# Attention and two feed-forward layers on one core: stores of parts one step later, behind the next step's loads

## The chip, the core and the metric

The kernel runs on one core of one Trainium2 chip. A core has five engines that run their own instruction streams in order and meet at semaphores: TensorE (PE in the rows; PEld is its weight load), VectorE (DVE), ScalarE (ACT), GpSimd (POOL) and SyncE (SP), which here issues every transfer between HBM and the core's memory. The metric is the device time of one execution in microseconds (us); lower is better.

## What is computed

Eight batches of eight heads of attention without a softmax over scores: q is softmaxed over its 64 features, k over its 576 positions, and the output is q (k^T v). The result, as 4608 tokens of 512 features, goes through two feed-forward layers of width 2048.

```python
def _attn_ref(q, k, v):                                   # (8, 8, 576, 64) each
    q_s = np.exp(q - np.max(q, axis=-1, keepdims=True))
    q_s = q_s / (np.sum(q_s, axis=-1, keepdims=True) + 1e-09)
    k_s = np.exp(k - np.max(k, axis=2, keepdims=True))
    k_s = k_s / (np.sum(k_s, axis=2, keepdims=True) + 1e-09)
    kv = np.einsum('bhsd,bhse->bhde', k_s, v)
    return np.einsum('bhsd,bhde->bhse', q_s, kv).astype(np.float32)

x = attn_out.transpose(0, 2, 1, 3).reshape(4608, 512)
h = x @ w_in;  x = (h - np.tanh(h)) @ w_out               # first layer
h = x @ w_in                                              # second layer, with a rational function
P = a[0] + a[1]*h + a[2]*h**2 + a[3]*h**3
Q = 1.0 + abs(b[0])*abs(h) + abs(b[1])*h**2
out = (P / (Q + 1e-6)) @ w_out
```

## The kernel before

Values are split in two parts, high and low, so that a product is three matmuls (high x high, high x low, low x high). The tokens are cut into nine blocks of 512 (NBLK), the layer's width into 16 slices of 128 (KF); a step is one slice of one block.

**The stages.** Up to some 140 us the attention of the first block is made. Then come the 144 steps of the first layer (loop over n in STEPS, j = block, f = slice). In a step TensorE makes the first product of slice f (`first_product`) and the second product of the slice two steps back (`second_product1`), and in between pieces of the next block's attention. From some 930 us on the second layer runs over an order that is written out by hand (ORDER), on units that are loaded back from HBM.

**A step's code** issues, in this order: `front(work[n])`, the parts of the next block's attention that are due in this step, loads, VectorE, ScalarE and GpSimd work; the first product; `turn(work[n])`, their TensorE work; the tanh (L936), the subtraction t (L939), its high part gh (L327) and low part gl (L331); what follows the TensorE work; and last, from step 17 on, one piece of each "errand" in the list `todo`. Each engine runs its instructions in that order.

**The attention pieces.** For each head pair p = 0 to 3 of the next block: `kv_max` and `kv_squares` make maxima of k and store them in HBM (kd, L532); `kv_fetch` loads them back, spread over the partitions, into the tile ke (L538); `kv_join` takes the maximum (mx<-ke, L544), `kv_sub` subtracts it from k into ke (L473), `kv_exp` takes the exponential (L483), and `kv_mm` multiplies with v (kvps, L490). For p = 1 the load is due in step 5, L544 and L473 in step 6, L483 and L490 in step 7; for p = 2 in steps 8, 9 and 10. The tile ke exists once. The parts of q go through HBM in the same way (qd, L622; ql, L629), and q's result is written to the four quarters of the tile xr in steps 5, 8, 11 and 14.

**The errands.** One (`errands`) brings the second layer's weights: a fetch into a staging tile raw (three of them; L118, L120), decoding on ScalarE and VectorE, splitting into high part e (three tiles) and low part m (four), and stores to HBM (L221, L225). The others are `x2_units`, one for each block that the first layer has done: step 1 copies the block's result from the accumulators to two staging tiles, and in steps 1 to 8 seven units of it are made in eight pieces. Each unit is split: a copy to a new high tile (ScalarE, L356), a subtraction in place (GpSimd, L357), and the stores of both parts (SyncE, L359), which are issued right there:

```python
hi = two(new_hi())                                        # one of the decoder's three e tiles
ACT.copy(out=hi.bitcast(F32R), in_=x)
POOL.tensor_tensor(out=x.bitcast(F32R), in0=x, in1=f32(hi), op=ALU.subtract)
for i, t in enumerate((hi, x)):
    SP.dma_start(out=two(x2d[j][:, 2 * UNITS.index(m) + i]), in_=f32(t))
```

SyncE issues in program order: a transfer whose data isn't ready holds all that stand behind it.

Of the kernel before, what the change touches and what calls it, by code (L numbers as in the profile page):

```python
# [8 lines left out]
F32 = mybir.dt.float32  # L9
F32R = mybir.dt.float32r  # L10
# [5 lines left out]
ALU = mybir.AluOpType  # L16
AX = mybir.AxisListType

P = 128
NB = 512  # L20
# [23 lines left out]
def attention_moe_moe2_kernel(ctx, tc, q, k, v, w1, w2, w3, w4, ca, cb, out):  # L44
# [21 lines left out]
    decp = tc.alloc_tile_pool(name="decp", bufs=2, side="right")  # L66
# [7 lines left out]
    PE, ACT, DVE, POOL, SP = nc.tensor, nc.scalar, nc.vector, nc.gpsimd, nc.sync  # L74

    def f32(ap):
        return ap.bitcast(F32)
# [111 lines left out]
    UNITS = (1, 5, 2, 6, 7, 4, 3)  # L189
    HALF = NB // 2  # L190

    def keep(key, n):
        parked[key] = dp.tile([P, n, NB], F32, tag=f"w{key}", name=f"w{key[0]}{key[1]}d")
        return parked[key]

    def errands():


        def raw():
            piece, t = staged.pop(0)  # L200
            return (t, *(dec_open(t) if wide else (None, t)))

        def whole(t, e, m):
            if wide:
                dec_join(e, m)
                return e, m
            e, m = (decp.tile([P, NB], x, tag=g, name=g, bufs=n) for x, g, n in ((U32, "e", 3), (U32, "m", 4)))
            POOL.tensor_copy(out=f32(m), in_=t)
            return e, m

        def high(e, m, n=NB):
            ACT.copy(out=e.bitcast(F32R)[:, 0:n], in_=f32(m)[:, 0:n])

        def low(e, m, n=NB):
            lo = m.bitcast(F32R)[:, 0:n]
            DVE.tensor_tensor(out=lo, in0=f32(m)[:, 0:n], in1=f32(e)[:, 0:n], op=ALU.subtract)

        def store(d, at, e, m, half):

            for i, x in enumerate((e, m)):  # L220
                SP.dma_start(out=d[:, UNITS.index(at), i * HALF:(i + 1) * HALF], in_=f32(x)[:, half * HALF:(half + 1) * HALF])  # L221

        def store_whole(d, e, m):
            for i, x in enumerate((e, m)):
                SP.dma_start(out=d[:, i], in_=f32(x))  # L225

        for f in range(0, KF, 2):
            d = keep(("a", f), len(UNITS))
            o = raw()
            fetch_w(1)  # L230
            yield
            e1, m1 = whole(*o)
            yield
            o = raw()
            high(e1, m1)
            fetch_w(1)
            yield
            e2, m2 = whole(*o)
            m4, m3 = (decp.tile([P, NB], U32, tag="m", name="m", bufs=4) for _ in range(2))
            x1, x2, x3, x4 = (f32(x) for x in (m1, m2, m3, m4))  # L240
            lo, hi = slice(0, HALF), slice(HALF, NB)
            POOL.tensor_tensor(out=x4[:, hi], in0=x1[:, lo], in1=x2[:, lo], op=ALU.subtract)
            POOL.tensor_tensor(out=x2[:, lo], in0=x2[:, lo], in1=x2[:, hi], op=ALU.add)
            POOL.tensor_tensor(out=x4[:, lo], in0=x2[:, lo], in1=x1[:, lo], op=ALU.subtract)
            POOL.tensor_tensor(out=x3[:, lo], in0=x1[:, hi], in1=x4[:, lo], op=ALU.subtract)
            yield
            high(e2, m2)
            low(e1, m1)
            store(d, 1, e1, m1, 0)
            store(d, 2, e1, m1, 1)  # L250
            yield
            low(e2, m2)
            store(d, 5, e2, m2, 0)
            store(d, 4, e2, m2, 1)
            e1 = decp.tile([P, NB], U32, tag="e", name="e", bufs=3)
            high(e1, m4)
            yield
            low(e1, m4)
            store(d, 6, e1, m4, 0)
            store(d, 7, e1, m4, 1)  # L260
            e2 = decp.tile([P, NB], U32, tag="e", name="e", bufs=3)
            high(e2, m3, HALF)
            yield
            low(e2, m3, HALF)
            store(d, 3, e2, m3, 0)
            for i in range(2):
                o = raw()
                yield
                e, m = whole(*o)
                fetch_w(1)  # L270
                yield
                high(e, m)
                yield
                low(e, m)
                store_whole(keep(("b", f + i), 2), e, m)

    todo = [errands()]

    def unpark(which, f):
# [26 lines left out]
    xr = xp.tile([P, KC, NB], F32, tag="xr", name="xr")  # L306
# [8 lines left out]
    def first_product(f):  # L315
        hps = ps_h.tile([P, NB], F32, tag="h", name="hps")
        for c in range(KC):
            wh, wl = wa(f, c)
            mm3(hps, wh, wl, xh[:, c, :], xl[:, c, :], c == 0, c == KC - 1)
        return hps  # L320
# [22 lines left out]
    def two(t):  # L343
        return t.rearrange("p (c x) -> p c x", c=2)

    def x2_units(j, k0, k1, ta, tb, new_hi):

        x11, x12, x21, x22 = k0[:, :, LO], k0[:, :, HI], k1[:, :, LO], k1[:, :, HI]
        ta, tb = two(ta), two(tb)

        def minus(o, a, b):
            POOL.tensor_tensor(out=o, in0=a, in1=b, op=ALU.subtract)

        def split(m, x):
            hi = two(new_hi())
            ACT.copy(out=hi.bitcast(F32R), in_=x)  # L356
            POOL.tensor_tensor(out=x.bitcast(F32R), in0=x, in1=f32(hi), op=ALU.subtract)  # L357
            for i, t in enumerate((hi, x)):
                SP.dma_start(out=two(x2d[j][:, 2 * UNITS.index(m) + i]), in_=f32(t))  # L359

        minus(ta, x12, x11)
        yield
        split(1, x11)
        minus(tb, x22, ta)
        yield
        split(5, ta)
        minus(x12, x22, x12)
        yield
        split(3, x22)
        yield  # L370
        split(7, x12)
        minus(ta, x21, tb)
        yield
        split(2, x21)
        yield
        split(6, tb)
        yield
        split(4, ta)

    identity = const.tile([P, P], F32, name="identity")  # L380
    coef = const.tile([P, 6], F32, name="coef")
# [278 lines left out]
    def front(todo):  # L660
        for fn, args in todo:
            if not isinstance(fn, tuple):
                fn(*args)
# [17 lines left out]
    for j in range(1, NBLK):  # L681
        for p in range(NPAIR):
            at = (j - 1) * KF + 3 * p
# [14 lines left out]
    with tc.manual_schedule():  # L698
# [56 lines left out]
        def second_product1(j, f, gh, gl):  # L755
            if f == 0:
                new_acc()
            wh, wl = wb(f)
            for m in range(4):
                c = slice(m * P, (m + 1) * P)  # L760
                mm3(acc[m], wh[:, c], wl[:, c], gh, gl, f == 0, f == KF - 1)

            def leave(acc=dict(acc)):
                halves = [xr[:, m:m + 2, :] for m in (0, 2)] if j == NBLK - 1 else [staging().rearrange("p (m t) -> p m t", m=2) for _ in range(2)]
                for m in range(4):
                    (DVE.tensor_copy if m % 2 else ACT.copy)(out=halves[m // 2][:, m % 2], in_=acc[m])
                if j < NBLK - 1:
                    todo.append(x2_units(
                        j, *halves, xr[:, 2, :], xr[:, 3, :],
                        lambda: decp.tile([P, NB], F32, tag="e", name="e", bufs=3),  # L770
                    ))

            return leave if f == KF - 1 else None

# [127 lines left out]
        for n in range(STEPS):  # L902
            j, f = n // KF, n % KF
            leave = None
            front(work[n])
            hps = first_product(f)
            if f == KF - 1 and j + 1 < NBLK:
                next_x()
# [3 lines left out]
            if n == last + 10:  # L912
                for errand in todo:
                    for _ in errand:
                        pass
                for pool in (att, bdp, decp, rawp):
                    pool.release()
                outp = ctx.enter_context(tc.tile_pool(name="outp", bufs=4, side="right"))
                rp = ctx.enter_context(tc.tile_pool(name="rp", bufs=2, side="right"))
                xup = ctx.enter_context(tc.tile_pool(name="xup", bufs=1, side="right"))  # L920
                units = [xup.tile([P, NB], F32R, tag=f"u{k}", name=f"u{k}") for k in range(12)]
                units += [w[:, c, :] for w in (xh, xl) for c in range(KC)]
                sums = xup.tile([P, NB], F32, tag="sums", name="sums")
                top = xup.tile([P, HALF], F32, tag="top", name="top")
                temp = xup.tile([P, NB], F32, tag="temp", name="temp")
                for u in range(6):
                    load_unit(0, u)
# [64 lines left out]
        for i in range(PAIRS + LAGS):  # L992
            for name, lag in ORDER:
                if 0 <= i - lag < PAIRS:
                    steps[name](i - lag)
                if i == 0 and name in ("P1", "P6"):
                    old()
            if i % 4 == 3:
                next(prep, None)

# [28 lines left out]
```

## Time and profile before

| | |
|---|---|
| median of 3 runs | 1704.54 us (1703.94 to 1705.71) |
| the profiled execution | 1705.21 us, its span 1703.4 us |
| busy, share of the span | TensorE 1644.1 us (97%), VectorE 1154.1 (68%), GpSimd 1035.3 (61%), ScalarE 1024.3 (60%) |
| TensorE busy, 0 to 140 us | 110.90 us |
| TensorE busy, 140 to 820 us | 660.90 us of 680 |
| TensorE busy, 820 to 920 us | 100.00 us of 100 |
| TensorE busy, 920 to 1703 us | 772.26 us of 783 |

The rows come from one profiled execution. A row of a view in order of time has a start (us from the span's start), a length, the engine and line, what is written and read, and in brackets how long the engine was idle before it and what ended that. "SPq" is an issue on SyncE's queue. Matmuls are pipelined and their ends are modelled.

### The profile page before, as it was taken

What the parts mean: (1) busy time and instruction counts of PE and PEld (TensorE: products, weight loads), DVE (VectorE), ACT (ScalarE), POOL (GpSimd) and SP (SyncE); (2) the same over time, 40 slices, a digit from 0 to 9 for tenths busy, and PEclk for the clock granted to TensorE, in tenths of its full rate; (3) what the DMA queues carried; (4) which work ended last, traced back from release to release, by engine and by line L of the source; (5) the groups of instructions that cost most, each with busy time, mean ns of one, the idle gap of its engine ahead of it and who ended that gap; (6) DMA issues with size and microseconds to landing.
All of it is one profiled execution on the core that took longest, in us unless ns stands there. A gap on an engine that the chain in (4) does not pass through costs nothing.

```text
span 1703.4 us, 25967 instructions
## 1 busy us (share of the span) xinstructions
PE 1644.1 (97%) x8776; PEld 1414.4 (83%) x8776; DVE 1154.1 (68%) x1948; ACT 1024.3 (60%) x1825; POOL 1035.3 (61%) x875
## 2 busy tenths in 40 slices
PE   5899999999999999999999999999999999999998
PEld 4677787888887788788888889998999999989996
DVE  7987566675756556654211778787878787878787
ACT  5675444544444444444332777777777777777775
POOL 4223626454553635446251888888888778878886
PEclk9999999999999999999999999999999999999999
DMA  8552654747375563735078676767675757676640
GB/s 221 169 169 87 191 161 150 203 125 218 117 198 148 153 200 121 204 93 167 13 237 300 251 268 221 271 213 271 211 272 198 260 198 260 200 258 204 218 153 26
DMA packets 246117, 323.69 MB, mean 190 GB/s; under 512 B 119008, under 2 KB 176352, under 8 KB 236768
## 3 DMA queue, kind: packets, MB, share of 16 engines
q1 hardware_dynamic: 245984, 322.03, 58.9%
q8 instruction: 69, 1.13, 0.3%
q14 instruction: 64, 0.52, 0.1%
HBM read 249.04 MB, written 72.93 MB: 189 GB/s over the span
## 4 chain that ended last, share of the span: by engine, by line
PE 75%; DVE 9%; DMA 5%; ACT 4%; issue 3%; POOL 2%; SPq 2%; ACTq 0%; POOLq 0%; DVEq 0%
PE acc L80 12%; PE acc L81 12%; PE acc L82 12%; PE z L826 12%; PE y L826 9%; PE hps L80 5%; PE hps L82 5%; PE hps L81 5%; DMA ke<-kd 2%; PE kvps L490 1%; DMA u<-x2d 1%; SPq L629 1%; DVE m L147 1%; DMA ql<-qd 1%; ACT m L133 1%
## 5 line engine op out<-in xcount | busy, mean ns | idle before, releaser
L331 POOL TENSOR_TENSOR gl<-t,gh 128x512 fp32r<-128x512 f32 x128 | 173.6, 1356 | 329.1 <-ACT gh L327 299.2
L327 ACT CAST gh<-t 128x512 fp32r<-128x512 f32 x128 | 79.9, 624 | 297.9 <-PE acc L82 122.0
L883 POOL TENSOR_TENSOR n<-n,r 128x512 f32<-128x512 f32 x144 | 186.7, 1296 | 97.2 <-ACT r L880 91.9
L883 POOL TENSOR_TENSOR n<-n,n 128x512 f32<-128x512 f32 x144 | 187.0, 1299 | 35.7 <-ACT n L867 35.7
L883 POOL TENSOR_TENSOR n<-n,h 128x512 f32<-128x512 f32 x144 | 187.6, 1303 | 9.7 <-DMA xh<-x2d 9.6
L939 DVE TENSOR_TENSOR t<-hps,t 128x512 f32<-128x512 f32 x128 | 87.5, 684 | 153.2 <-ACT t L936 152.7
L936 ACT ACTIVATE t<-hps 128x512 f32<-128x512 f32 x144 | 86.0, 597 | 95.7 <-PE hps L82 75.9
L837 ACT COPY sums<-z 128x256 f32<-128x256 f32 x144 | 53.9, 374 | 134.0 <-PE z L826 134.0
L863 ACT ACTIVATE n<-h,coef 128x512 f32<-128x512 f32 x144 | 116.9, 812 | 0.3 <-POOL n L883 0.3
L893 DVE CAST gh<-a 128x512 fp32r<-128x512 f32 x144 | 99.6, 692 | 16.8 <-PE acc L82 1.4
L896 DVE TENSOR_TENSOR gl<-a,gh 128x512 fp32r<-128x512 f32 x144 | 99.7, 692 | 15.2 <-DVE gh L893 0.5
L872 DVE SCALAR_TENSOR_TENSOR a<-h,absb,a 128x512 f32<-128x512 f32 x144 | 107.6, 747 | 3.0 <-ACT a L857 2.9
L889 DVE SCALAR_TENSOR_TENSOR a<-a,n 128x512 f32<-128x512 f32 x144 | 100.0, 695 | 14.0 <-POOL n L883 8.1
L857 ACT ACTIVATE a<-h,coef 128x512 f32<-128x512 f32 x144 | 100.7, 699 | 2.5 <-DVE gl L896 2.5
L886 DVE SCALAR_TENSOR_TENSOR a<-a,r 128x512 f32<-128x512 f32 x144 | 99.4, 690 | 0.8 <-ACT r L880 0.8
L875 ACT ACTIVATE r<-a,bias_q 128x512 f32<-128x512 f32 x144 | 97.3, 676 | 0.0
L880 ACT ACTIVATE r<-r 128x512 f32<-128x512 f32 x144 | 91.3, 634 | 4.6
L860 ACT ACTIVATE h<-h 128x512 f32<-128x512 f32 x144 | 89.4, 621 | 1.3 <-DMA xh<-x2d 0.8
L598 POOL TENSOR_TENSOR qe<-qe,qs 128x512 f32<-128x512 f32 x36 | 38.6, 1072 | 64.2 <-DVE qs L597 64.2
L490 PE MATMUL kvps<-vt,ke 128*128 128x130 f32 x320 | 49.1, 306 | 27.5 <-ACT ke L483 25.9
L490 PEld LDWEIGHTS kvps<-vt,ke 128*128 128x128 f32 x320 | 44.9, 212 | 35.2 <-ACT ke L483 31.7
L636 DVE TENSOR_TENSOR ql<-ql,qh 128x512 fp32r<-128x512 f32 x28 | 23.5, 841 | 74.2 <-ACT qh L635 74.2
(360 smaller groups left out, 5295.9 us busy)
## 6 DMA issues: line engine op xcount, KB each, us to landing
u<-x2d SPq DMA_DIRECT2D x78, 256.0 KB, 5.4
raw<-in_moe_w_in_dram SPq DMA_DIRECT2D x32, 512.0 KB, 4.4
raw<-in_moe_w_out_dram SPq DMA_DIRECT2D x32, 512.0 KB, 4.4
x2d<-e SPq DMA_DIRECT2D x56, 256.0 KB, 3.1
wa0h<-wa0d SPq DMA_DIRECT2D x9, 1024.0 KB, 5.1
wa1h<-wa2d SPq DMA_DIRECT2D x9, 1024.0 KB, 5.1
wa2h<-wa4d SPq DMA_DIRECT2D x9, 1024.0 KB, 5.2
wa3h<-wa6d SPq DMA_DIRECT2D x9, 1024.0 KB, 7.4
```

What stands on the lines that cost most here:

```text
L80: PE.matmul(o, lhi, rhi, start=start, stop=False)
L81: PE.matmul(o, lhi, rlo, start=False, stop=False)
L82: PE.matmul(o, llo, rhi, start=False, stop=stop)
L331: eng.tensor_tensor(out=gl, in0=g, in1=f32(gh), op=ALU.subtract)
L490: PE.matmul(ps[:, 0:2 * (D + 1)], e[:, g].rearrange("p h d -> p (h d)"), vs[:, :, g, :], start=g == 0, stop=g == G - 1,)
L826: PE.matmul(o, w, x[:, xc], start=m in (1, 5) and c == k == 0, stop=c == 1 and k == 2, skip_group_check=True,)
L857: ACT.activation(out=new(t, "a", ps_a), in_=t["h"], func=AF.Abs, scale=b0)
L863: ACT.activation(out=new(t, "n1"), in_=t["h"], func=AF.Identity, scale=a3, bias=a2)
L872: DVE.scalar_tensor_tensor(out=t["a"], in0=t["h2"], scalar=b1, in1=t["a"], op0=ALU.mult, op1=ALU.add)
L883: return lambda t: POOL.tensor_tensor(out=t[a], in0=t[a], in1=t[b], op=op)
L889: DVE.scalar_tensor_tensor(out=t["a"], in0=t["a"], scalar=2.0, in1=t["n0"], op0=ALU.subtract, op1=ALU.mult)
L896: DVE.tensor_tensor(out=t["g"][1], in0=t["a"], in1=f32(t["g"][0]), op=ALU.subtract)
```

## The change

The stores of the x2 units and of the second layer's weights are no longer issued where the parts are made. `send` puts them in a list, and `flush` issues that list: in each step right behind `front(work[n])`, that is behind the next step's attention loads; where all errands are finished (step `last + 10`), after each piece; and in the second layer's loop every fourth pair. The high parts of x2 no longer take the decoder's e tiles: of a block's seven, three go to quarters 0 and 1 of xr (`free`), and four to quarters of the two staging tiles whose units have been split before (x11, x22, x11 and x12).

```diff
+    late = []
+
+    def send(out, in_):
+        late.append(lambda: SP.dma_start(out=out, in_=in_))
+
+    def flush():
+        while late:
+            late.pop(0)()
...
             for i, x in enumerate((e, m)):
-                SP.dma_start(out=d[:, UNITS.index(at), i * HALF:(i + 1) * HALF], in_=f32(x)[:, half * HALF:(half + 1) * HALF])
+                send(d[:, UNITS.index(at), i * HALF:(i + 1) * HALF], f32(x)[:, half * HALF:(half + 1) * HALF])
...
             for i, x in enumerate((e, m)):
-                SP.dma_start(out=d[:, i], in_=f32(x))
+                send(d[:, i], f32(x))
...
-    def x2_units(j, k0, k1, ta, tb, new_hi):
+    def x2_units(j, k0, k1, ta, tb, free):
...
-        def split(m, x):
-            hi = two(new_hi())
+        def split(m, x, hi=None):
+            hi = two(free()) if hi is None else hi
             ACT.copy(out=hi.bitcast(F32R), in_=x)
-            POOL.tensor_tensor(out=x.bitcast(F32R), in0=x, in1=f32(hi), op=ALU.subtract)
+            POOL.tensor_tensor(out=x.bitcast(F32R), in0=x, in1=hi, op=ALU.subtract)
             for i, t in enumerate((hi, x)):
-                SP.dma_start(out=two(x2d[j][:, 2 * UNITS.index(m) + i]), in_=f32(t))
+                send(two(x2d[j][:, 2 * UNITS.index(m) + i]), t)
...
-        split(3, x22)
+        split(3, x22, x11)
         yield
         split(7, x12)
         minus(ta, x21, tb)
         yield
-        split(2, x21)
+        split(2, x21, x22)
         yield
-        split(6, tb)
+        split(6, tb, x11)
         yield
-        split(4, ta)
+        split(4, ta, x12)
...
-                    todo.append(x2_units(
-                        j, *halves, xr[:, 2, :], xr[:, 3, :],
-                        lambda: decp.tile([P, NB], F32, tag="e", name="e", bufs=3),
-                    ))
+                    free = [xr[:, c, :] for c in (1, 1, 0)]
+                    todo.append(x2_units(j, *halves, xr[:, 2, :], xr[:, 3, :], free.pop))
...
             front(work[n])
+            flush()
             hps = first_product(f)
...
                 for errand in todo:
                     for _ in errand:
-                        pass
+                        flush()
+                flush()
...
             if i % 4 == 3:
+                flush()
                 next(prep, None)
```

On SyncE, ahead of the load of ke for the pair p = 1 in the second block's steps (step 5, the load ahead of the stop at 199 us), there stood before:

```order
105 L120 DMA raw<-in_moe_w_out_dram 128x512
106 L359 DMA x2d_98<-e 128x512
107 L359 DMA x2d_98<-xr 128x512
108 L622 DMA qd_1781<-qe 128x512
109 L532 DMA kd_1788<-mc 128x4
110 L359 DMA x2d_98<-e 128x512
111 L359 DMA x2d_98<-raw 128x2x256
112 L538 DMA ke<-kd_1610 128x512
113 L428 DMA vt_176<-in_v_dram 128x4x64 x2
114 L431 DMA vt_176<-in_v_dram 64x2x64
```

and now:

```order
105 L120 DMA raw<-in_moe_w_out_dram 128x512
106 L631 DMA qd_1777<-qe 128x512
107 L541 DMA kd_1784<-mc 128x4
108 L199 DMA x2d_98<-xr 128x512 x2
109 L547 DMA ke<-kd_1610 128x512
110 L437 DMA vt_176<-in_v_dram 128x4x64 x2
111 L440 DMA vt_176<-in_v_dram 64x2x64
112 L199 DMA x2d_98<-raw 128x2x256 x2
```

The two stores of the unit split in step 4 (rows 110 and 111 before) stand behind the loads of ke and v now (row 112); those of step 3 (106 and 107) are what is left ahead of ke (108).

The pair p = 2 in the fifth block's steps (step 8, the load ahead of the stop at 514 us), on SyncE before:

```order
367 L359 DMA x2d_101<-e 128x512
368 L359 DMA x2d_101<-raw 128x2x256
369 L622 DMA qd_4745<-qe 128x512
370 L532 DMA kd_4752<-mc 128x4
371 L120 DMA raw<-in_moe_w_out_dram 128x512
372 L359 DMA x2d_101<-e 128x512
373 L359 DMA x2d_101<-xr 128x512
374 L538 DMA ke<-kd_4560 128x512
```

and now:

```order
354 L199 DMA x2d_101<-xr 128x512
355 L199 DMA x2d_101<-raw 128x2x256
356 L631 DMA qd_4717<-qe 128x512
357 L541 DMA kd_4724<-mc 128x4
358 L199 DMA x2d_101<-raw 128x2x256 x2
359 L120 DMA raw<-in_moe_w_out_dram 128x512
360 L547 DMA ke<-kd_4535 128x512
```

The fetch of raw weights stays ahead of the load of ke, with the two stores of step 6 ahead of both; those of step 7 stand behind. The fetch now goes to a staging tile that the decoder reads in the same step.

On ScalarE in the second block, from the tanh of step 6 to the front of step 7; before:

```order
200 L936 ACTIVATE t<-hps 128x512
201 L327 CAST gh<-t 128x512
202 L212 CAST e<-m 128x512
203 L356 CAST e<-raw 128x512
204 L483 ACTIVATE ke<-ke 128x640
205 L635 CAST qh<-ql 128x512
```

and now:

```order
200 L945 ACTIVATE t<-hps 128x512
201 L336 CAST gh<-t 128x512
202 L221 CAST e<-m 128x512
203 L365 CAST raw<-raw 128x2x256
204 L492 ACTIVATE ke<-ke 128x640
205 L644 CAST qh<-ql 128x512
```

Nothing moved here: the copy of the unit's high part stays right ahead of the exponential, and goes to a quarter of a staging tile instead of an e tile.

## Rows read from the trace of the kernel before

**Rows 1.** who TensorE waits for: 140 to 820 us, then 820 us to the end.
```profile
PE kvps L490 <- ACT ke L483: 16.6, 6, 4.0
...
PE acc L80 <- DVE gh L893: 3.0, 3, 1.1
```

**Rows 2.** TensorE in order of time, stops at L490 (start, length, ... [idle before <-releaser]).
```profile
199.49 0.59 PE L490 MATMUL kvps<-vt,ke 128*128 128x130 f32 x1 [4.00 <-ACT ke L483]
...
299.47 0.38 PE L490 MATMUL kvps<-vt,ke 128*128 128x130 f32 x1 [2.37 <-ACT ke L483]
...
513.90 0.58 PE L490 MATMUL kvps<-vt,ke 128*128 128x130 f32 x1 [3.10 <-ACT ke L483]
...
595.29 0.55 PE L490 MATMUL kvps<-vt,ke 128*128 128x130 f32 x1 [3.03 <-ACT ke L483]
...
696.67 0.38 PE L490 MATMUL kvps<-vt,ke 128*128 128x130 f32 x1 [3.34 <-ACT ke L483]
```

**Rows 3.** windows of 20 us: length, busy time by engine, granted clock, DMA share, GB/s.
```profile
200.00:220.00 20.00, 20.00 (x92) 17.01 (x91) 13.29 (x24) 9.90 (x19) 9.10 (x8) 0.93 0.78 232
...
300.00:320.00 20.00, 20.00 (x100) 16.74 (x99) 13.04 (x21) 8.72 (x17) 9.54 (x8) 1.00 0.75 210
...
500.00:520.00 20.00, 16.90 (x74) 14.01 (x73) 10.71 (x18) 9.61 (x19) 10.68 (x10) 0.91 0.69 190
...
580.00:600.00 20.00, 16.97 (x76) 14.19 (x75) 11.48 (x19) 8.06 (x16) 13.30 (x12) 0.91 0.70 204
...
680.00:700.00 20.00, 16.42 (x73) 13.18 (x72) 10.50 (x21) 9.92 (x19) 11.05 (x9) 0.94 0.78 230
```

**Rows 4.** ScalarE in order of time, at S1.
```profile
197.14 0.62 ACT L327 CAST gh<-t 128x512 fp32r<-128x512 f32 x1 [6.38 <-DVE t L939]
```

**Rows 5.** VectorE in order of time, the maximum over ke (L544) at five stops.
```profile
192.91 1.10 DVE L544 TENSOR_REDUCE mx<-ke 128x128 f32<-128x512 f32 x1 [3.93 <-DMA ke<-kd]
...
293.41 1.09 DVE L544 TENSOR_REDUCE mx<-ke 128x128 f32<-128x512 f32 x1 [4.76 <-DMA ke<-kd]
...
507.29 1.12 DVE L544 TENSOR_REDUCE mx<-ke 128x128 f32<-128x512 f32 x1 [3.13 <-DMA ke<-kd]
...
587.69 1.11 DVE L544 TENSOR_REDUCE mx<-ke 128x128 f32<-128x512 f32 x1 [3.65 <-DMA ke<-kd]
...
689.43 1.10 DVE L544 TENSOR_REDUCE mx<-ke 128x128 f32<-128x512 f32 x1 [4.38 <-DMA ke<-kd]
```

**Rows 6.** SyncE's queue in order of time, ahead of S1 (start of issue, its length).
```profile
180.25 0.32 SPq L532 DMA_DIRECT2D kd<-mc  x1
...
188.46 0.37 SPq L359 DMA_DIRECT2D x2d<-raw  x1
188.92 0.42 SPq L538 DMA_DIRECT2D ke<-kd  x1
```

**Rows 7.** the tile ke: ns min/median/max of L473, first and last start; landing of its loads.
```profile
L473 DVE TENSOR_TENSOR ke<-kt,mx x24: 824/826/1945, 169.4 to 723.8; 128x640 f32<-128x640 f32 x24
...
DMA to landing us min/median/max: 3.4/4.2/5.2
```

**Rows 8.** SyncE and ScalarE in order of time, ahead of S2, S4, S5 and S6.
```profile
283.28 0.32 SPq L532 DMA_DIRECT2D kd<-mc  x1
...
499.45 0.79 ACT L133 ACTIVATE m<-raw 128x512 uint16<-128x512 uint32 x1
...
580.14 0.33 SPq L120 DMA_DIRECT2D raw<-in_moe_w_out_dram  x1
...
679.58 0.32 SPq L532 DMA_DIRECT2D kd<-mc  x1
```

**Rows 9.** VectorE and GpSimd in order of time, at S4 and at S1.
```profile
508.44 1.95 DVE L473 TENSOR_TENSOR ke<-kt,mx 128x640 f32<-128x640 f32 x1
...
508.41 1.30 POOL L357 TENSOR_TENSOR xr<-xr,e 128x512 fp32r<-128x512 f32 x1
...
190.08 1.29 POOL L357 TENSOR_TENSOR raw<-raw,e 128x512 fp32r<-128x512 f32 x1
```

## The prediction

> **What bounds the kernel now.** First the busy table: TensorE is busy nearly throughout, so a change that adds and removes no matmul can only win TensorE's idle time, or stretches in which its clock is low. Next, who TensorE waits for. In the second stage (140 to 820 us, eight blocks of 16 steps) nearly all is one line: the product that makes a head pair's K-V matrix, L490, waits for ScalarE's exponential, L483, 16.6 us in six stops, while from 820 us on the largest group is 3.0 us [rows 1]. I call the stops S1 to S6; five have their rows, of 4.00, 2.37, 3.10, 3.03 and 3.34 us, at 199, 299, 514, 595 and 697 us [rows 2], and S3 (395 us) is what is left of the sum, 0.76 us. Then the clock: in the windows behind four of them the granted clock has a mean of 0.91 to 0.94, and behind S2 it stays at 1.00 [rows 3]. TensorE has two levels, 1.2 and 2.4 GHz, so these are short stretches at the lower one after stops of 3.0 us and more; a stop of 2.4 us had none.
>
> Now back along S1. ScalarE sits 6.38 us idle until VectorE's subtraction of the step before is done (t, L939), and the exponential stands three instructions behind that [rows 4]. VectorE is in order, and ahead of L939 stands the maximum over ke (L544), which waited 3.93 us for the load of ke; at the other stops it waited 4.76, 3.13, 3.65 and 4.38 us [rows 5]. And the load was late because of its place on SyncE's queue: kd leaves at 180.25, then come the two stores of an x2 unit, of which the one of the low part waits for GpSimd's subtraction and leaves only at 188.46; ke's load is issued right behind, at 188.92 [rows 6]. The load needs nothing of that store.
>
> **The change, term by term.** (1) Stores move behind the next step's loads. The rows of the changed order show what stands between kd and ke then: at S1 two stores, both of the step before, whose subtractions are long done; the store that blocked now stands behind ke's load and three loads of v. SyncE takes 0.46 us from one issue to the next (188.46 to 188.92 [rows 6]) and ke lands a median 4.2 us after its issue, 3.4 to 5.2 [rows 7]. So:
> S1: kd ends at 180.57, two stores 0.9, issue at 181.5, landing at 185.7. VectorE is free at 192.91 - 3.93 = 188.98 [rows 5], so its whole wait of 3.93 goes, of a stop of 4.00.
> S2: kd ends at 283.60 [rows 8]; six stores stand between (four weight parts, two x2 parts), 2.8 us; issue 286.4, landing 290.6 instead of 293.4: 2.8 earlier, so all 2.37 go.
> S3: 0.76 us; the same store is ahead of it, and it goes.
> S4: here a fetch of raw weights stays ahead of ke, and it newly waits until the decoder has read the staging tile that it refills (x2 now keeps both its staging tiles longer, so the third is taken). That read, L133, ends at 499.45 + 0.79 = 500.24 [rows 8]; fetch, then ke at 500.7, landing 504.9 instead of 507.3: 2.4 of 3.10.
> S5: the fetch ahead of ke waits in the same way today and leaves at 580.14 [rows 8]; ke at 580.5, landing 584.7 instead of 587.7: 2.9 of 3.03 (VectorE is free at 584.04).
> S6: kd ends at 679.90 [rows 8], six stores 2.8, issue 682.7, landing 686.9 instead of 689.4: 2.5 of 3.34.
> Sum 14.9 us; bounds 0 (nothing moves) and 16.6. What is late next at S1 is the exponential itself: it then ends at about 195.5, and TensorE is there at 195.5.
>
> (2) Where VectorE lands. Moved up, its two-input subtraction L473 meets GpSimd's work. In S4's row it took 1.95 us beside a GpSimd subtraction that began 0.03 us before it, and its median over 24 is 0.83 [rows 7, 9]: a price of 0 to 1.12 us each. At S1 it would begin at 188.98 + 1.10 = 190.1, just as GpSimd's L357 starts (190.08 [rows 9]): 1.1 us. For the other five, one of which meets such work today, I take 0.3 together, an estimate. That makes 1.4, bounds 0 and 6.7. The Trainium skill, "SBUF — State Buffer", section "Who interferes with whom", says that a VectorE instruction with two SBUF inputs contends with a GpSimd one that reads SBUF, and that the one that comes second waits the whole of the other out; by that rule, the 1.95 agrees. It speaks against moving VectorE into GpSimd's busy stretches, and I carry it as a rival below.
>
> (3) The clock. Lost work per window is its length times one minus the granted share: 20 us x 0.07, 0.09, 0.09 and 0.06 [rows 3] are 1.4 + 1.8 + 1.8 + 1.2 = 6.2 us. What is left of each stop by (1) and (2) is at most 1.2 us, under S2's 2.37, which had no drop; so I take all 6.2, bounds 0 and 6.2. The Trainium skill, "TensorE: Matmul & The Clock Gate", section "Part 1: The HAM clock gate (the "warmup" mystery)", says that for modelling the ramp is under 1% of a typical span and not worth fitting. By that the term would be left out and the time come out at 1692.0; the rows price it at a third of the gain, and they decide.
>
> (4) High parts in free quarters. Same number of copies (ScalarE), subtractions (GpSimd) and stores. Three of seven high parts of a block go to quarters of xr, four to quarters of the staging tiles that x2 has finished with. The decoder's e tiles are no longer shared; at S1 that frees nothing on the path, since the next tanh waits for GpSimd's low part anyway. New are waits of ScalarE's copies for stores of what they overwrite. The closest is the copy of step 6, which stands right ahead of the exponential: it overwrites x22, whose low part's store could leave at 188.46 today [rows 6] and leaves behind ke and v then, at about the same time. With ke's landing of 3.4 to 5.2 us it is free by 191.9 to 193.7, and the copy comes a microsecond after gh, which moves from 197.1 [rows 4] to 193.2: at about 194.3. Cost 0; without that cover each microsecond of lateness is one of stop. For the last block the stores wait up to four pairs longer in the third stage, where TensorE's largest waits add up to 3.0 us [rows 1]: 0.
>
> (5) Given back. The next head pair's product comes three steps later, without a stop but for S4, with TensorE now there sooner by the stop and the clock: 4.2 us after S1, 2.4, 0.8, 4.7 after S5, 3.4 after S6. Its ke load also stands behind a store today and moves up, at S4 by 2.4. If all move by only that, 1.8 + 2.3 + 1.0 = 5.1 us come back; if the others, with no fetch ahead, move by 4 or more, about 0. Take 1.0.
>
> Sum: 14.9 - 1.4 + 6.2 - 1.0 = 18.7 us. The profiled execution took 1705.2 us (its span is 1703.4, the rest lies around it), which gives 1686.5; the median of the runs is 0.7 lower, 1704.5, so the forecast is **1685.8**. The best case, all stops and all low clock, is 1704.5 - 16.6 - 6.2 = 1681.7.
>
> **Rivals.** A, the port: by the rule under (2), each of the six subtractions waits a whole GpSimd operation. 6 x 1.12 = 6.7 instead of 1.4, so 1691.1. For it speaks S4's row, against it that 0.83 is the median of all 24 [rows 7]. 12%.
> B, the stop moves on to the next pair: if those loads don't move up at all, the whole lead is given back, 4.2 + 2.4 + 0.8 + 4.7 + 3.4 = 15.5 us instead of 1.0: 1700.3. Against it: the same blocking store goes from ahead of them too. 8%.
> C, no change: the load of ke is freed, but the exponential is held as long by something else on ScalarE or VectorE at that time; or the flushed stores, bunched ahead of the load, hold its data back. 1704.5. Against it: VectorE's wait is directly on the load in all rows [rows 5], and no load of ke took over 5.2 us to land, whatever ran ahead of it [rows 7]. 8%.
> D, slower: the in-place high copy of step 6 waits for the store that frees its target. It decides from the point where that store lands later than the copy comes today (about 198 us at S1), over 9 us after its issue; two microseconds beyond that in six blocks are 12 us: 1716. Against it is the landing of 3 to 5 us. 5%.
>
> **How the numbers follow.** The forecast's own case holds 67%: 1681.7 to 1690, with the bounds of (2) and (5). With A and most of B the range is 1681 to 1699; it leaves out C, D and the tail of B, some 17%. A measurement of this kernel can tell some 0.2%, 3.4 us, from no change: faster is the forecast, A and B, 87%; the same is C, 8%; slower is D, 5%.
>
> **What would show it.** In the changed kernel's profile: ke's loads issued within 1 to 3 us of kd at S1, S2 and S6; the VectorE wait at L544's successor in line under 1 us at S1 and at most 2.5 elsewhere; TensorE's wait for the exponential in 140 to 820 us at 2 to 5 us instead of 16.6; a granted clock of 1.00 in all windows there; the second stage ending some 19 us sooner and the third unchanged. Wrong would be: a stop of over 2 us at step 10 of a block (B), L473 at 1.5 us and more in most rows (A), ScalarE idle until the landing of an x2d store (D).

## The result, and the profile after

The changed kernel takes **1678.84 us** (median of four runs, 1678.46 to 1680.47), the kernel before 1705.12 us (four runs, 1703.94 to 1708.39). The ratio is 0.9845, with a 95% interval of 0.9828 to 0.9862: 26.3 us gained, by the interval 23.5 to 29.3. Forecast were 18.7 us, 1685.8, with a range of 1681 to 1699. The sign and the mechanism came as forecast, the size did not: the time lies 2.2 us below the range.

The profiled execution of the changed kernel took 1680.47 us, the slowest of its four, with a span of 1678.6 us, 24.8 less than the 1703.4 before. What the traces can account for is these 24.8.

First who TensorE waits for from 140 to 820 us, in the changed kernel (us in total, times, longest). L499 was L490, L492 was L483:

```profile
PE kvps L499 <- ACT ke L492: 2.2, 3, 1.2
```

Of 16.6 us in six stops [rows 1] 2.2 are left. Two of the stops are still of note, S1 and S6, here in order of time:

```profile
197.74 0.71 PE L499 MATMUL kvps<-vt,ke 128*128 128x130 f32 x4 [0.81 <-ACT ke L492]
...
674.51 0.71 PE L499 MATMUL kvps<-vt,ke 128*128 128x130 f32 x4 [1.20 <-ACT ke L492]
```

The windows of the changed kernel, one of 680 us and those behind S1 and S6 (length, busy time of TensorE, its weight loads, VectorE, ScalarE, GpSimd, granted clock, DMA share, GB/s); [rows 3] had 0.91 to 0.94 there:

```profile
140.00:820.00 680.00, 676.19 (x3150) 564.64 (x3149) 425.91 (x699) 326.46 (x598) 347.63 (x279) 1.00 0.55 157
...
197.00:217.00 20.00, 19.26 (x96) 16.43 (x97) 13.41 (x22) 10.09 (x21) 10.84 (x9) 1.00 0.83 235
...
672.00:692.00 20.00, 18.80 (x90) 15.50 (x89) 13.28 (x22) 11.17 (x22) 11.44 (x9) 1.00 0.94 267
```

SyncE's queue at S1 in the changed kernel, to be laid beside [rows 6] (start, length of the issue):

```profile
182.10 0.32 SPq L541 DMA_DIRECT2D kd<-mc  x1
182.51 0.86 SPq L199 DMA_DIRECT2D x2d<-xr  x2
183.47 0.41 SPq L547 DMA_DIRECT2D ke<-kd  x1
183.93 1.28 SPq L437 DMA_DIRECT2D vt<-in_v_dram  x2
...
185.99 4.70 SPq L199 DMA_DIRECT2D x2d<-raw  x2
190.78 1.34 SPq L638 DMA_DIRECT2D ql<-qd  x2
```

ke's load leaves 1.37 us behind kd instead of 8.67; the store that blocked it (it is the group that takes until 190.69) now stands behind the loads of ke and v. VectorE, GpSimd and ScalarE at the same place:

```profile
189.07 1.77 DVE L225 TENSOR_TENSOR m<-m,e 128x512 fp32r<-128x512 f32 x1 [2.58 <-POOL m L254]
190.76 1.11 DVE L553 TENSOR_REDUCE mx<-ke 128x128 f32<-128x512 f32 x1
191.90 0.83 DVE L482 TENSOR_TENSOR ke<-kt,mx 128x640 f32<-128x640 f32 x1
...
188.99 1.30 POOL L366 TENSOR_TENSOR raw<-raw 128x512 fp32r<-128x512 f32 x1
...
191.96 1.93 POOL L366 TENSOR_TENSOR raw<-raw,xr 128x512 fp32r<-128x512 f32 x1
...
195.39 0.62 ACT L336 CAST gh<-t 128x512 fp32r<-128x512 f32 x1 [2.76 <-DVE t L948]
...
196.44 0.61 ACT L365 CAST raw<-raw 128x512 fp32r<-128x512 f32 x1
196.95 0.73 ACT L492 ACTIVATE ke<-ke 128x640 f32<-128x640 f32 x1
```

The maximum over ke has no wait any more, where it had 3.93 us [rows 5]; ScalarE's idle time ahead of gh falls from 6.38 us [rows 4] to 2.76.

**Where the 24.8 us went.** In the six blocks of steps from the second to the seventh TensorE runs the same 2688 instructions in the same order in both traces, so the time from each start to the next can be compared one by one. The sums of the blocks fall from 598.5 to 573.8 us; the rest of the program is unchanged in sum.

| us | forecast | in the traces |
|---|---|---|
| stops at the K-V product, terms (1), (2) and (5) | 14.9 - 1.4 - 1.0 = 12.5 | 14.6 |
| stretches at the lower clock, term (3) | 6.2 | 6.3 |
| everything else, 3.1 of it at q's product | 0 | 3.9 |
| sum | 18.7 | 24.8 |

### The profile page after: what moved, and what is told of

Its sections match the earlier page's. It is cut to its first block, busy times and chain, and to the rows that moved or that the text cites. A ratio compares the mean times of both kernels' runs of the same rounds, so it can differ in the third digit from the quotient of the medians.

```text
span 1678.6 us, 25941 instructions
## 1 busy us (share of the span) xinstructions
PE 1633.4 (97%) x8776; PEld 1407.5 (84%) x8776; DVE 1165.0 (69%) x1948; ACT 1022.7 (61%) x1825; POOL 1041.8 (62%) x875
## 4 chain that ended last, share of the span: by engine, by line
PE 83%; DVE 7%; ACT 4%; DMA 3%; issue 1%; SPq 1%; POOL 0%; DVEq 0%; ACTq 0%; POOLq 0%
PE acc L80 14%; PE acc L81 14%; PE acc L82 14%; PE z L833 12%; PE y L833 9%; PE hps L82 6%; PE hps L80 6%; PE hps L81 6%; PE kvps L499 1%; DMA u<-x2d 1%; DMA ke<-kd 1%; ACT m L133 1%; DVE m L147 1%; DVE m L134 1%; DVE ke L482 1%
## 5 line engine op out<-in xcount | busy, mean ns | idle before, releaser
L340 POOL TENSOR_TENSOR gl<-t,gh 128x512 fp32r<-128x512 f32 x128 | 177.2, 1385 | 328.3 <-ACT gh L336 299.4
L851 DVE TENSOR_TENSOR h<-y,sums 128x256 f32<-128x256 f32 x72 | 30.5, 424 | 58.7 <-PE y L833 58.7
L855 DVE TENSOR_TENSOR h<-y,top 128x512 f32<-128x512 f32 x72 | 49.7, 690 | 25.6 <-ACT top L844 25.4
L645 DVE TENSOR_TENSOR ql<-ql,qh 128x512 fp32r<-128x512 f32 x28 | 27.3, 976 | 49.8 <-ACT qh L644 44.6
```

The costliest lines, as they stand in the source:

```text
L340: eng.tensor_tensor(out=gl, in0=g, in1=f32(gh), op=ALU.subtract)
```

## The experiments

Two questions were open: what the 3.9 us are that no term held, and whether the edit that I had costed at nothing, the quarters, is worth nothing. The kernel before had a median of 1706.2 to 1706.3 us in the three groups of runs that follow, and each ratio is to the runs of its own group.

### Each part of the change alone

The quarters without the late stores (`quarters_now`):

```diff
     def send(out, in_):
-        late.append(lambda: SP.dma_start(out=out, in_=in_))
+        SP.dma_start(out=out, in_=in_)
```

> The second part of the change alone: x2's high parts go to the free quarters, but all stores are issued at once, as before. Theory: the gain comes from SyncE's order alone; ke's load still stands behind the store of a low part, so the stops of 14.6 us and the low clock of 6.3 us stay: 1705 us, within 1 of the kernel before. Rival: a part of what the forecast missed comes from the decoder's e tiles being free sooner: 1699 to 1703.

Measured: 1706.79 us, ratio 1.0001 (0.9991 to 1.0011), 17.5 us of waits for the exponential. The quarters alone give nothing, as the theory had it.

The late stores without the quarters (`late_e_tiles`):

```diff
-        split(3, x22, x11)
+        split(3, x22)
...
-                    free = [xr[:, c, :] for c in (1, 1, 0)]
-                    todo.append(x2_units(j, *halves, xr[:, 2, :], xr[:, 3, :], free.pop))
+                    todo.append(x2_units(j, *halves, xr[:, 2, :], xr[:, 3, :],
+                        lambda: decp.tile([P, NB], F32, tag="e", name="e", bufs=3)))
```

> The first part alone: stores one step later, x2's high parts still in the decoder's three e tiles, which are then held until the later store has landed. Theory: the tiles are free before the next high part needs them, so the time is that of the full change, 1679 us, within 1.5. Rival: a tile held a step longer makes ScalarE's copy or the decoder wait for a store's landing, some 1 to 2 us in most blocks, right ahead of the exponential: 1685 to 1692.

Measured: 1715.15 us, ratio 1.0057 (1.0037 to 1.0076): slower than the kernel before, and some 36 us slower than the full change. Both my theories fell; the rival had the right mechanism at a quarter of its size. Who waits, in `late_e_tiles`, 140 to 820 us:

```profile
PE kvps L499 <- ACT ke L492: 28.4, 10, 5.3
...
ACT e L365 <- DMA x2d<-e: 17.2, 18, 2.6
...
ACT e L221 <- DMA wa0d<-e: 5.8, 2, 3.8
```

ScalarE's copies and decoding into an e tile wait for the landing of the store that frees it, with all parts of the weights some 70 us together; in the kernel before these waits were 1.2 us. At S1 of `late_e_tiles`, SyncE and ScalarE:

```profile
195.20 0.44 SPq L199 DMA_DIRECT2D wa0d<-e  x1
...
196.16 0.45 SPq L199 DMA_DIRECT2D wa0d<-e  x1
...
198.62 0.62 ACT L221 CAST e<-m 128x512 fp32r<-128x512 f32 x1 [3.77 <-DMA wa0d<-e]
199.69 0.62 ACT L365 CAST e<-raw 128x512 fp32r<-128x512 f32 x1 [0.46 <-DMA x2d<-e]
200.22 0.73 ACT L492 ACTIVATE ke<-ke 128x640 f32<-128x640 f32 x1
```

The two stores of a high part of the weights (a half of the tile each), put off, leave at 195.20 and 196.16; the e tile that they read is the next that ScalarE needs, it waits for both, and the exponential stands two instructions behind. ke's load was early (issued at 182.29); what replaced the wait for it is a wait for a buffer.

To see whether it is the tile's holding, and not the tiles as such, `e_tiles_low_late` keeps the e tiles, but puts off only the stores of low parts. In both `store` functions and in `split`, i is 0 for the high part:

```diff
-    def send(out, in_):
-        late.append(lambda: SP.dma_start(out=out, in_=in_))
+    def send(out, in_, i):
+        if i:
+            late.append(lambda: SP.dma_start(out=out, in_=in_))
+        else:
+            SP.dma_start(out=out, in_=in_)
```

> As late_e_tiles (x2's high parts in the decoder's e tiles), but only the low parts' stores go a step later; the high parts' stores, x2's and the weights', are issued at once, so that an e tile comes free as early as in the kernel before. Theory: late_e_tiles lost its 36 us because a copy to an e tile waits for the landing of the late store that frees it; with these stores early again the waits go, and what blocked SyncE, the low parts' stores, stays late: 1681 us, at most 1686. Rival: the high parts' stores block SyncE as well (they wait for ScalarE's copy, behind tanh and gh), and half or more of the gain stays lost: 1692 to 1703.

Measured: 1679.65 us, ratio 0.9845 (0.9831 to 0.9859), beside 1679.25 and 0.9838 for the unedited change in the same group. Its waits:

```profile
PE kvps L502 <- ACT ke L495: 3.3, 5, 1.3
...
ACT e L368 <- DMA x2d<-e: 0.3, 1, 0.3
```

17.2 us of the waits for x2's stores became 0.3. So the quarters are not a gain of their own: they pay for holding buffers longer, and not holding them pays as well. SyncE does wait for ScalarE's copies of x2's high parts here, 27 times and 56.0 us in all from 140 to 820 us, and issuing these stores at once still cost nothing that can be measured: it was enough to put off the low parts, which wait for GpSimd (x2) or VectorE (weights). The high parts put off alone were not run.

### Whose stores

`late_x2_only` issues the weights' stores at once and puts off x2's alone:

```diff
             for i, x in enumerate((e, m)):
-                send(d[:, i], f32(x))
+                SP.dma_start(out=d[:, i], in_=f32(x))
```

(and the same in `store`.)

> The changed kernel with the stores of the weights' parts issued at once, as before; only x2's stores go a step later. Theory: what blocks SyncE is the store of x2's low part, which waits for GpSimd; the weights' parts are ready when their stores come, and those cost the loads only SyncE's 0.46 us each: 1679 to 1682 us. Rival: the weights' stores hold the loads as well (the low part m waits for VectorE), and a third or more of the gain is lost: 1687 to 1692.

Measured: 1680.76 us, ratio 0.9852 (0.9837 to 0.9868), against 1680.45 and 0.9849 of the changed kernel in the same group (`after_again`).

> The changed kernel itself, unedited, beside the three that follow on one chip, so that they can be set against it: 1679 us, within 1 (its first four runs had 1678.46 to 1680.47).

The gain comes with x2's stores; for the weights' stores none can be measured. The trace of `late_x2_only` (its slowest execution, 1682.97 us) does show them at S6: four of the weights' stores still stand ahead of ke there, the first low part is late, ke's load leaves 4.64 us behind kd instead of 3.36, and TensorE waits 1.94 us instead of 1.20, with the lower clock behind it (columns as above):

```profile
673.58 0.49 PE L499 MATMUL kvps<-vt,ke 128*128 128x130 f32 x2 [1.94 <-ACT ke L492]
...
673.00:693.00 20.00, 19.42 (x85) 16.33 (x86) 15.87 (x24) 10.62 (x20) 10.21 (x8) 0.91 0.90 264
```

### Which loads

Where the flush stands decides which loads pass the stores. It stood behind the loads only in the steps that load ke (`late_ke_only`), and only in those that load ql (`late_ql_only`, with 0 in place of 2):

```diff
+            if f % 3 not in (2,):
+                flush()
             front(work[n])
-            flush()
+            if f % 3 in (2,):
+                flush()
```

> The stores go behind the next step's loads only in the steps that load ke (f = 2, 5, 8, 11 of a block, in three steps one); elsewhere they go ahead of them, as before, so the loads of q's part ql stand behind them again. Both theories see all stops and the low clock gone, 14.6 and 6.3 us. They differ on the 3.8 us beyond, most of it waits of q's product (xps) for the parts of bd. Theory K: those waits follow from late ke, they go too: 1679 us. Theory Q: they follow from late ql, they stay: 1682.6 us, and the pitch from one matmul of xps to the next is as long as in the kernel before.

> The mirror image: the stores go behind the next step's loads only in the steps that load ql (f = 0, 3, 6, 9, 12, 15), so ke's loads stand behind the blocking stores as before. Theory K: 1705 us, nothing gained. Theory Q: the waits of q's product go, the stops stay: 1701.3 us. In both, TensorE waits 14 to 17 us for the exponential in 140 to 820 us.

Measured: 1690.39 us, ratio 0.9905 (0.989 to 0.9919), and 1699.6 us, ratio 0.9954 (0.9934 to 0.9974). The second is theory Q's number within 2 us. What decides for Q is the trace: with ql alone moved up, the comparison of starts has 3.1 us less at q's product, the same as in the full change, while the stops for the exponential stay (15.7 us). The six blocks take 5.1 us less in all; the other 2 are stops and stretches at the lower clock that came out otherwise, so that the agreement of the time is in part chance (its runs lie between 1693.4 and 1701.6 us). For the first, Q's direction held and both numbers were missed, by 8 and 11 us. Who TensorE waits for in `late_ke_only`:

```profile
PE xps L80 <- ACT bd01h L519: 3.8, 2, 3.0
...
PE kvps L499 <- ACT ke L492: 0.4, 1, 0.4
```

The stops at the K-V product are gone and have come up at q's product, one step on. SyncE there, from ke's load to ql's:

```profile
592.15 0.58 SPq L547 DMA_DIRECT2D ke<-kd  x1
...
594.78 0.59 SPq L199 DMA_DIRECT2D wa10d<-e  x1
...
603.82 0.44 SPq L199 DMA_DIRECT2D x2d<-xr  x1
604.35 2.01 SPq L638 DMA_DIRECT2D ql<-qd  x3
```

Twelve stores, those of two steps, stand between: put off in one step and not in the next, they bunch ahead of ql, which is then later than it ever was. I had not counted that, so this run does not price ke's part by itself; it shows that the two loads need the same treatment.

The wait that I had not seen runs in the kernel before as follows (waits, 140 to 820 us; then around 498 us VectorE, ScalarE and TensorE):

```profile
DVE ql L636 <- ACT qh L635: 71.7, 25, 4.9
...
ACT qh L635 <- DMA ql<-qd: 29.4, 17, 3.3
```

```profile
492.93 0.63 ACT L635 CAST qh<-ql 128x512 fp32r<-128x512 f32 x1 [1.87 <-DMA ql<-qd]
...
493.59 0.69 DVE L636 TENSOR_TENSOR ql<-ql,qh 128x512 fp32r<-128x512 f32 x1 [3.34 <-ACT qh L635]
...
497.51 0.15 DVE L501 TENSOR_SCALAR rs<-kvps 128x1 f32<-128x1 f32 x1
...
498.21 0.63 ACT L510 ACTIVATE bd11h<-kvps,rs 64x64 fp32r<-64x64 f32 x2
...
498.89 0.36 PE L80 MATMUL xps<-qh,bd11h 128*128 128x192 f32 x1 [0.49 <-ACT bd11h L510]
```

ScalarE waits for the load of ql, VectorE for ScalarE's high part of it, and behind VectorE's subtraction stand, in order, what is due next, down to the sums (L501) from which ScalarE makes the parts of bd, the scaled K-V matrix, that q's product (xps) needs. In the changed kernel the first two waits are these:

```profile
DVE ql L645 <- ACT qh L644: 44.6, 23, 3.7
...
ACT qh L644 <- DMA ql<-qd: 3.8, 4, 1.2
```

### What the clock is worth by itself

`before_filled` is the kernel before with TensorE kept at work in the four stops behind which the clock fell:

```diff
+    FILL = {(2, 1): 13, (5, 2): 12, (6, 1): 12, (7, 1): 13}
+
     def kv_mm(b, p):
...
         ps = pool.tile([P, NB], F32, tag=tag, name="kvps")
+        for _ in range(FILL.get((b, p), 0)):
+            PE.matmul(ps, wsl["a", 0][0][:, 0, 0:P], xh[:, 0, :], start=True, stop=True)
```

> The kernel before with TensorE kept at work in the four stops that a low clock follows: ahead of kvps in S1, S4, S5 and S6 13, 12, 12 and 13 needless products of 128x512 (0.227 us each, 2.7 to 3.0 us) go into the same bank, which the first real product overwrites. The stops don't end sooner, since ke is as late as before. Theory: the low clock of 6.3 us comes from TensorE's idleness and goes with it; 1705.1 - 6.3 = 1698.8 us, granted clock 1.00 in the windows behind the stops. Rival: it comes from something else about these places and stays: 1705 us.

Measured: 1699.38 us, ratio 0.9964 (0.9949 to 0.998): 6.9 us gained between the medians, with fifty products of no use added. The windows behind the four stops, each from about where its stop ends (columns as above):

```profile
198.00:218.00 20.00, 19.47 (x98) 16.58 (x99) 12.87 (x22) 9.67 (x19) 10.15 (x9) 1.00 0.77 232
508.00:528.00 20.00, 19.63 (x98) 16.33 (x97) 9.96 (x19) 10.06 (x20) 5.14 (x4) 1.00 0.74 202
588.00:608.00 20.00, 19.10 (x91) 15.59 (x89) 11.21 (x21) 9.29 (x19) 9.82 (x9) 1.00 0.81 239
691.00:711.00 20.00, 18.96 (x90) 15.68 (x91) 13.54 (x21) 9.78 (x19) 10.24 (x8) 1.00 0.81 212
```

The granted clock is 1.00 in all four. So the lower clock there came of TensorE's idleness, and term (3) is shown apart from the stops. From start to start the stretches behind the four stops are 6.1 us shorter in this trace (6.2 forecast, 6.3 in the changed kernel), while the stops, six old and two new, are 2.3 us longer in sum, 1.6 of it at the next pair behind S5 (a wait of 1.46 us at 609.58). The traces' spans differ by 5.8 us; what the 6.9 of the medians has beyond that is within the scatter.

### A little more

At S6 six flushed stores still stand between kd and ke. In the changed kernel:

```profile
659.00 0.32 SPq L541 DMA_DIRECT2D kd<-mc  x1
...
661.35 0.90 SPq L199 DMA_DIRECT2D x2d<-xr  x2
662.36 0.39 SPq L547 DMA_DIRECT2D ke<-kd  x1
```

`late_ke_ql` flushes ahead of the stores of kd and qd, and behind the loads of ke and ql; it is the diff of `late_ke_only` with (0, 2).

> The changed kernel with the flush moved in one step of three: in the steps that store kd and qd (f = 1, 4, 7, 10, 13) the late stores go ahead of these instead of behind, so that ke's load, a step later, finds only the stores of one errand less between kd and itself; in the steps that load ql and ke they go behind the loads as in the changed kernel. Theory: at S6 ke's load, issued at 662.36 behind six stores that take 2.8 us, is issued some 2.5 sooner and the 1.2 us left there go: 1677.5 us against 1679 of the changed kernel. Rival: kd and qd themselves are held by a low part that is not ready, and the loads with them: 1683 to 1690.

> The changed kernel itself beside the next one, with more rounds: 1680 us, within 1.

> The kernel late_ke_ql once more, with more rounds, since it stood only 2.1 us under the changed kernel. Its trace had S6's wait gone, 1.5 us less between the starts of TensorE's products in the six blocks; so 1678.5 us, 1.5 under after_third, within 1. Rival: the difference was scatter, and the two agree within 0.5 us.

Measured: 1678.32 us beside 1680.45, and with more rounds 1677.32 (ratio 0.9825, 0.9811 to 0.9838) beside 1679.25 (0.9838, 0.9825 to 0.9852). SyncE at S6 in `late_ke_ql`:

```profile
657.22 0.32 SPq L541 DMA_DIRECT2D kd<-mc  x1
657.64 0.37 SPq L547 DMA_DIRECT2D ke<-kd  x1
```

The stop at S6 is gone, and the starts in its six blocks add up to 1.6 us less than in the trace of `after_again` (1.9 less than in the changed kernel's first). Twice the median is about 2 us lower, as the trace says it should be; the intervals overlap, so by the runs alone it is not settled. (The times came 0.8 us above the first forecast and 1.2 below the second, which allowed 1; `after_again` missed its forecast by 1.5 us, with 1 allowed, and `after_third` kept it.) It is the fastest of the kernels here.

## Why the prediction was too small

**The bound.** Right: a late load of ke behind a transfer whose data wasn't ready, in all six stops, and the clock behind four of them. That this transfer is the store of an x2 low part holds for S1, where SyncE waited 5.3 us for GpSimd ahead of ke, but not for all. What SyncE waited for longest in the kernel before, ahead of S4 (498 to 504 us), S5 (576 to 584) and S6 (678 to 686):

```profile
SPq L359 <- ACT e L356: 3.3, 1, 3.3
...
SPq L120 <- DVE m L134: 2.9, 1, 2.9
...
SPq L221 <- DVE m L216: 2.2, 1, 2.2
```

At S4, and with 2.6 us at S3, it was the store of x2's high part, with 1.0 for the low part behind it; at S5 the fetch of raw weights, as the prediction had it; at S6, and with 2.3 at S2, the store of a low part of the weights, which waits for VectorE. The sums of term (1) hold all the same, since they count what is left between kd and ke.

**Term (1), the loads of ke.** Right to 0.5 us: 14.9 of 16.6 were to go, 14.4 went by the waits. The queue was worked out well too: kd to ke 1.25 us forecast at S1 and 1.37 measured, 3.1 and 3.36 at S6. What stayed late at S1 (0.81 us) is the exponential, as named; gh, ahead of it, came at 195.39 us and not at 193.2, in a trace whose second stage begins 1.0 us later.

**Term (2), VectorE beside GpSimd.** 1.4 forecast, 1.1 of it at S1. At S1 the two subtractions do meet, 0.06 us apart, but VectorE's came first and took its 0.83 us; GpSimd's took 1.93 instead of the 1.30 of the one before it. I had worked the starts out to 0.1 us and put VectorE second; the sign of so small a difference can't be forecast, and a bet of even chances, about half of 1.1 at S1, was all that it was worth. At S5 and S6 VectorE did come second: L482 took 1.41 us (570.47) and 1.20 (668.02), 0.58 and 0.37 over its median (S5 had paid in the kernel before too, 1.44 us at 588.84, where the prediction counts S4 alone). S5 has 0.1 us of a stop left even so; the 0.37 lie on the chain to the 1.20 left at S6. Rival A, 1.12 at all six, didn't come: L482 has a median of 826 ns over 24 in the changed kernel and a largest of 1908. Its condition, that VectorE comes second each time, was wrong.

What I had not priced is a meeting that the kernel before has too: VectorE's L225, which began at 189.07, 0.08 us behind GpSimd's L366, took 1.77 us instead of its median of 0.68. It stands right ahead of the maximum over ke, so by these rows its 1.09 us are more than the 0.81 left at S1; no run takes them away, and this stays an estimate. The rule of the Trainium skill on "SBUF — State Buffer" ("Who interferes with whom") agrees with both rows at S1, also where it says that issue order and not the shape of an operation decides who is blocked. The one that came second paid 0.63 of the 0.77 us that the other still had to run, and 1.09 of 1.22.

**Term (3), the clock.** Right, and shown alone. It was read a little short: two windows of [rows 3] hold only a part of their stretch. Windows that begin at the stops show 0.91 at S1 (199 to 219 us) and at S6 too, where [rows 3] had 0.93 and 0.94:

```profile
697.00:717.00 20.00, 20.00 (x90) 16.66 (x89) 14.18 (x23) 9.76 (x19) 9.35 (x8) 0.91 0.85 223
```

By the prediction's own sum that is 4 x 1.8 = 7.2 us. Its reason for taking the whole term, that what is left of each stop is under S2's 2.37 us, was weaker than it looks, since the length of a stop doesn't settle it: the clock fell behind stops of 2.64 and 2.71 us in `quarters_now` (0.91 in the windows from 300 and 597 us) and of 1.94 in `late_x2_only`, and stayed behind one of 2.72 in `late_ql_only` (1.00 from 586 us). The sentence of the Trainium skill ("TensorE: Matmul & The Clock Gate", "Part 1: The HAM clock gate (the "warmup" mystery)") that for modelling the ramp costs under 1% of a typical span speaks of a share of the whole span, and 6.3 of 1705 us is indeed 0.4%; against an edit that gains 26 it is a quarter, and without it the forecast would have missed by 13 us instead of 7.

**Term (4), the quarters.** Costed at 0, and 0 by itself (1.0001); but I asked only what the quarters cost, not what the late stores cost without them. They take away 36 us. A kin of that mechanism was in the text, as rival D at 1716 us: a copy that waits for the store that frees its target. With the e tiles it happens, at 1715; that the numbers agree is chance, since D priced 2 us in each of six blocks behind one late landing, and here copies and decoding wait 39 times, some 70 us, for stores that were issued late. In the quarters the copy at S1 comes without a wait, as term (4) had it, though at 196.44 and not at 194.3.

**Term (5), given back.** 1.0 forecast, 0 measured: no product of a pair p = 2 has a stop of note in the changed kernel. Rival B fell with it.

**What was not in the sum.** The traces gave 24.8 us and the sum 18.7. Of the 6.1 between, 2.1 are what terms (2) and (5) took off and the stops did not lose, and 3.9 were in no term; 3.1 of these are at q's product, and they are the step that failed. The prediction put at nothing, without a reason, every load but ke's that the late stores let through: its term (1), "stores move behind the next step's loads", followed the queue only as far as ke. The load of ql (L629) stands on the same queue behind the same stores, and the two rows above, 29.4 and 71.7 us of waits, were there to be read. `late_ql_only` shows that the 3.1 us go with ql alone; the other 0.8 I can't place. The rows looked harmless, since the list of TensorE's waits has 0.7 us for q's product. But that list counts idle time, and the ends of matmuls are modelled: at 498.89 it shows 0.49 us idle, where the times from start to start show 0.80 us for this matmul and 0.42 for the one two behind, against 0.15 and 0.11 in the changed kernel. It understates each stop by some 0.16 us too (a matmul of 512 columns is drawn 0.39 us long and followed by the next after 0.227). For the same reason the best case, 1681.7, was no bound: it added up only what one line of that list held and the clock, and the range ended 0.7 us below it.

**What is left open.** The sum of the terms is 24.8 us for the two profiled executions; the medians differ by 26.3 in the first group, and by 25.8 and 27.0 for the same kernel in the two others. The 1 to 2 us beyond the traces I can't place; the runs of either kernel scatter by as much.

## What to carry to other kernels

When a store is moved behind loads, list every load that stood behind it, and follow each to its reader; the ones that don't show as idle time of the bounding engine count too, and are seen in the times from start to start. A store that is put off holds its buffer for as long: here it was enough to put off the parts whose data comes last and to let the others go at once, or else to give them buffers that nobody waits for. And where TensorE stands still, read the granted clock behind the stop and add what is lost there to the price of the stop.

## What the runs showed of the hardware

- Fifty needless products made the kernel 6.9 us faster (interval 3.4 to 8.7), since TensorE didn't fall to 1.2 GHz behind four idle stretches of 3.0 to 4.0 us. The length of such a stretch alone doesn't tell: the clock fell behind one of 1.94 us in `late_x2_only` and stayed at 2.4 GHz behind one of 2.72 in `late_ql_only`.
- Of two subtractions of VectorE and GpSimd that began 0.06 and 0.08 us apart, the later one paid each time: GpSimd 1.93 us instead of 1.30, VectorE's L225 1.77 instead of its median of 0.68, some 0.14 us less than the rest of the other one's time.
- A store that lands in about 3 us cost ScalarE up to 4.7 us where it was put off: the wait is the delay of the issue and the landing together (at S1 of `late_e_tiles` 1.3 us until the issue at 196.16 and 2.5 from there to the copy).
